# POOL's subtraction for k in two halves; pair 2's centroid steps and the products of the turned w_out one slot later

## The chip, the cores and the metric

The kernel runs on one core of one Trainium2 chip. The metric is the device time of one execution in microseconds (us); 562.74, 564.26 and 565.34 us were measured for the kernel before, and their median is the time to beat. Names of engines: PE is TensorE, DVE is VectorE, ACT is ScalarE, POOL is GpSimd, SP is SyncE, which issues all DMAs here.

## The reference

Three layers follow each other: clustered attention, a layer with a rational activation, and a soft mixture of experts.

```python
# attention: B=2, H=8, S=768, D=64, 16 centroids a head
q_assign = np.argmax(np.einsum('bhsd,hcd->bhsc', q_n, c_n), axis=-1)     # and k_assign
mask = q_assign[:, :, :, None] == k_assign[:, :, None, :]
scores = np.where(mask, scale * np.matmul(q, k.transpose(0, 1, 3, 2)), -1e9)
attn = softmax(scores);  x = attn @ v                                    # -> [1536, 512]
# rational layer: d_ff = 2048
h = x @ w_in;  g = (a0 + a1*h + a2*h2 + a3*h3) / (1 + |b0|*|h| + |b1|*h2 + 1e-6);  x = g @ w_out
# soft mixture: 8 experts of 4 slots, F = 1024
logits = x @ phi;  slot_input = softmax_over_tokens(logits).T @ x
slot_out[e] = relu(slot_input[e] @ w1[e]) @ w2[e];  out = softmax_over_slots(logits) @ slot_out
```

## The kernel before

**The slots.** Attention is a loop over 96 slots, 12 for each of 8 pairs of heads (a pair is two heads of one batch, 2 x 64 rows). In slot n, PE turns (transposes) the exponentials of unit n (`turn`, L398, tile sT), then makes the scores of unit n+2 (`a1_mm`, L374 and L375, tile s), then the steps listed as "P" for this slot, then the product with v of an earlier group (`a2_av`, L411), then the steps listed as "T". DVE does its listed steps first ("D0", "D", "D1") and then the row minimum of the scores of unit n+2 (`a1_neg`, L383, tile e); ACT does the exponential of unit n+1 (L387) and copies the turned tile out (L404, eT), then its listed steps ("A"). POOL does only listed steps ("G0", "G"). Each list has (slot offset, engine, step) entries: a table written by hand sets the order on PE, ACT, DVE and POOL. The scores have one PSUM buffer, so L374 of a slot waits until DVE's L383 of the slot before has read it; sT has one too.

**The steps of a pair.** While a pair is in its 12 slots, `prep` prepares the pair two ahead; it is added at slot 4 of each pair (for pair 2 at slot 4 of the whole loop, so an entry with offset 1 stands in slot 5). `scores` (L230) multiplies raw q and k with the centroids, two halves c = 0 and 1; `scaled` (L235, ACT) scales them; `scT` (L249) turns them; `best` (L257, L258, DVE) finds the maximum; `first(0)` to `first(2)` (L266, L268, L271, DVE) make a one-hot (eq); `ohT`, `count`, `masks`, `nonhot`, `signed` and `alive` (L276, L284, L290 to L293, L298, L303, L311) make masks from it, and `qalive` (L315, DVE) applies one to q. `ksplit` rounds k on POOL (L239, ka) and subtracts the rounded part (L240, kb); six DMAs (L244) bring ka and kb to the operand tiles k1 and k2. `qsplit` (L325, L326) does the same with q.

**Small PSUM tiles.** All these small products, and those of the weights below, take tiles mf of one pool with three buffers (`m_tile`); a product that finds its buffer unread waits on its engine, and everything behind it on that engine waits too.

**The weights.** 32 blocks of w_in and w_out are decoded from 64-bit floats meanwhile (`decode_steps`: L521, L522, L528, L532 on DVE, L525 on ACT, L537 and L544, L545 on POOL). For each of the 16 blocks of w_out, `wphi_steps` turns the block (`tr`, L560), copies it (`tcopy`, L564, tile wT, ACT), multiplies it with phi (`mm`, L569), keeps the result (`keep_`, L576, DVE), and for every fourth block turns and sums it (`fin`, L581; `total`, L584). Blocks start every 2.65 slots.

**Start and fillers.** Pair 0 is prepared ahead of slot -2 (`first_pair`). There the centroid norms end with L502 and L503 on DVE (tile pc), on which L235 waits. Products with a tile of zeros (`idle`, L478, tile rest) fill PE there and in slots up to 5.

**The rest.** L768 to L771 are the products with w_in, with the rational function on ACT, POOL and DVE; the last stage (L983 to L1074) makes the experts. There the order on PE for the experts' products is not written by hand: a scheduler orders L1074 (products with w2), L1038 (sums of slot outputs, tile SO, copied and split by DVE at L1040 and L1042) and L1049 (output products). The order of SP's DMAs is the scheduler's too.

Of the kernel before, what the change touches and what calls it, by code (L numbers as in the profile page):

```python
# [8 lines left out]
F32 = mybir.dt.float32  # L9
# [5 lines left out]
ALU = mybir.AluOpType  # L15
# [43 lines left out]
def tile_kernel(ctx, tc, qT, kT, v, cenT, cenP, consts, constsb, ab, w_in, w_out, phi, w1, w2, out, dbg=None):  # L59
    nc = tc.nc  # L60
    PE, ACT, DVE, POOL, SP = nc.tensor, nc.scalar, nc.vector, nc.gpsimd, nc.sync
# [5 lines left out]
    HS = S // 2  # L67
# [80 lines left out]
    def m_tile(dt=F32):  # L148
        if dt == BF16:
            return psM.tile([128, 1024], BF16, tag="m", name="mb")  # L150
        return psM.tile([128, 512], F32, tag="m", name="mf")

    def first_pair(r, o, f):

        hold = f["hold"]

        def nonhot_k(h):
            m = psS[h].tile([128, 2, 512], F32, tag="S", name="s1")
            for c in range(2):
                PE.matmul(m[64:80, c, 0:HS], hold["W"][0:64, 160 + 16 * h:176 + 16 * h],  # L160
                          hold["oT"][0:64, c * HS:(c + 1) * HS], start=True, stop=True)
            ACT.activation(o[h]["k2"][64:80, :].rearrange("p (c n) -> p c n", c=2), m[64:80, :, 0:HS], AF.Copy, scale=-BIG)

        def nonhot_q(h, c):
            m = m_tile()
            w = slice(c * HS, (c + 1) * HS)
            PE.matmul(m[64:80, 0:HS], hold["W"][0:64, 128 + 16 * h:144 + 16 * h], hold["oT"][0:64, w], start=True, stop=True)
            ACT.copy(o[h]["q2"][64:80, w], m[64:80, 0:HS])

        def q0(h):  # L170
            w = slice(0, HS)
            q1, q2 = o[h]["q1"], o[h]["q2"]
            a, l = slice(64 * h, 64 * h + 64), slice(64 - 64 * h, 128 - 64 * h)
            qa = hold["qa", 0]
            ACT.copy(q1[a, w], qa[a, :])
            POOL.tensor_scalar(q2[0:64, w], qa[a, :], 1.0, 1.0, ALU.mult, ALU.mult)
            DVE.tensor_tensor(q1[l, w], qa[a, :], q1[a, w].bitcast(F32), ALU.subtract)

        def front():
            f["scores"](0)  # L180
            f["scores"](1)
            f["ksplit"]()
            idle(2)
            f["scaled"](0)
            f["scT"](0)
            f["best"](0)
            f["scaled"](1)
            f["scT"](1)
            f["best"](1)
            for i in range(3):  # L190
                f["first"](i)
            idle(12)
            f["ohT"]()
            f["count"]()
            idle(8)
            f["masks"]()

        def back():
            f["alive"](0)
            f["qalive"](0)  # L200
            nonhot_k(0)
            q0(0)
            nonhot_q(0, 0)
            q0(1)
            nonhot_k(1)
            nonhot_q(1, 0)
            idle(4)

        rest = [(0, "P", lambda: f["alive"](1)),
                (1, "D", lambda: f["qalive"](1)),  # L210
                (1, "G", lambda: f["qsplit"](1, slice(HS, S))),
                (1, "P", lambda: (nonhot_q(0, 1), nonhot_q(1, 1)))]
        return front, back, rest

    def prep(p):

        hp = p % (H // 2)
        r = raws.pop(p)
# [3 lines left out]
        def tile_(pool, tag, shape, dt):  # L222
            hold[tag] = pool.tile(shape, dt, tag=tag, name=tag)
            return hold[tag]

        def scores(c):
            m = hold["m", c] = m_tile()
            for g in range(4):
                a = slice(64 * (g % 2), 64 * (g % 2) + 64)
                PE.matmul(m[32 * g:32 * g + 32, 0:HS], cT[a, hp, :], r["qqkk"[g]][a, c * HS:(c + 1) * HS],  # L230
                          start=True, stop=True)

        def scaled(c):
            sc = hold["sc"] if c else tile_(t_p, "sc", [128, S], F32)
            ACT.activation(sc[:, c * HS:(c + 1) * HS], hold.pop(("m", c))[:, 0:HS], AF.Copy, scale=rn[:, hp:hp + 1])  # L235

        def ksplit():
            ka, kb = tile_(t_p, "ka", [128, S], F32R), tile_(t_p, "kb", [128, S], F32R)
            POOL.tensor_scalar(ka, r["k"], 1.0, 1.0, ALU.mult, ALU.mult)  # L239
            POOL.tensor_tensor(kb, r["k"], ka.bitcast(F32), ALU.subtract)  # L240
            for h in range(2):
                a = slice(64 * h, 64 * h + 64)
                for dst, src in ((o[h]["k1"][0:64, :], ka), (o[h]["k1"][64:128, :], ka), (o[h]["k2"][0:64, :], kb)):
                    SP.dma_start(dst.bitcast(F32), src[a, :].bitcast(F32))  # L244

        def scT(c):
            m = hold["m", c] = m_tile()
            for i in range(3):
                PE.transpose(m[:, i * 128:(i + 1) * 128], hold["sc"][:, (3 * c + i) * 128:(3 * c + i + 1) * 128], ident)  # L249

        def best(c):
            if c == 0:
                tile_(s2_p, "mx", [128, 6, 4], F32)
                tile_(t_p, "eq", [128, 6, 4, 16], BF16)
            mv = hold.pop(("m", c))[:, 0:HS].rearrange("p (i g c) -> p i g c", i=3, g=4)[:, :, :, 0:16]
            mc = hold["mx"][:, 3 * c:3 * c + 3, :]
            DVE.tensor_reduce(mc, mv, AX.X, ALU.max)  # L257
            DVE.tensor_tensor(hold["eq"][:, 3 * c:3 * c + 3], mv,  # L258
                              mc.unsqueeze(3).to_broadcast([128, 3, 4, 16]), ALU.is_equal)
# [72 lines left out]

        if p == 0:
            return first_pair(r, o, locals())
        return [
            (1, "T", lambda: scores(0)),
            (2, "A", lambda: scaled(0)),
            (2, "T", lambda: scores(1)),
            (3, "P", lambda: scT(0)),
            (3, "A", lambda: scaled(1)),  # L340
            (4, "D0", lambda: best(0)),
            (4, "P", lambda: scT(1)),
            (5, "D0", lambda: best(1)),
            (6, "D0", lambda: first(0)),
            (6, "G", ksplit),
            (7, "D0", lambda: first(1)),
            (8, "D0", lambda: first(2)),
# [128 lines left out]
    def idle(n):  # L476
        for _ in range(n):
            PE.matmul(rest_ps, zero[:, 0:128], zero, start=True, stop=True)  # L478
# [75 lines left out]
    def wphi_steps(f):  # L554

        def steps(hold):
            def tr():
                m = hold["m"] = m_tile()
                for c in range(NCC):
                    PE.transpose(m[:, c * 128:(c + 1) * 128], hold["w"][:, c * 128:(c + 1) * 128], ident)  # L560

            def tcopy():
                hold["wT"] = dec_p.tile([128, 512], F32, tag="wT", name="wT")
                ACT.copy(hold["wT"], hold.pop("m"))  # L564

            def mm():
                m = hold["m"] = m_tile()
                for c in range(NCC):
                    PE.matmul(m[32 * c:32 * c + 32, 0:128], ph[:, c, :], hold["wT"][:, c * 128:(c + 1) * 128],  # L569
                              start=True, stop=True)  # L570

            def keep_():
                k = f % 4
                if k == 0:
                    wph["t"] = dec_p.tile([128, 512], F32, tag="wph", name="wph")
                DVE.tensor_copy(wph["t"][:, k * 128:(k + 1) * 128], hold.pop("m")[:, 0:128])  # L576

            def fin():
                m = hold["m"] = m_tile()
                for k in range(4):  # L580
                    PE.transpose(m[:, k * 128:(k + 1) * 128], wph["t"][:, k * 128:(k + 1) * 128], ident)  # L581

            def total():
                DVE.tensor_reduce(wphi0[:, f - 3:f + 1, :], hold.pop("m").rearrange("p (k c s) -> p k s c", k=4, c=4),  # L584
                                  AX.X, ALU.add)

            return [(4, "P", tr), (5, "A", tcopy), (5, "T", mm), (6, "D1", keep_)] + \
                ([(6, "P", fin), (7, "D1", total)] if f % 4 == 3 else [])
        return steps

    w_in_w = w_in.bitcast(I32)
# [40 lines left out]
    manual.__enter__()  # L632
    start()
    front, back, rest = prep(0)
    SP.dma_start(ph, phi.rearrange("(c p) s -> p c s", p=128))
    SP.dma_start(coef, ab)
    steps = prep(1)
    front()
    early = [steps.pop(0)[2] for _ in range(5)]
# [8 lines left out]
    for n in range(-LEAD, NSL + 6):  # L648
        p, k = divmod(n, 12)
# [7 lines left out]
        if k == 4 and n > 0 and p + 2 < NP:  # L657
            add(n, prep(p + 2))
# [408 lines left out]
    for c0, cw in COLS:  # L1067
        ne = 256 // cw
        so = bank()
        for e in range(E):  # L1070
            wt = W["w2", e - e % ne, c0][0][:, (e % ne) * 8 * cw:]
            for kk in range(8):
                k = kk % 4
# [77 lines left out]
```

## Time and profile before

| what | value |
|---|---|
| median of three runs | 564.26 us (562.74 to 565.34) |
| the profiled execution's own time | 561.49 us |
| its span, first to last instruction | 559.7 us |
| busy: PE, DVE, ACT, POOL | 528.1, 425.9, 380.5, 275.4 us |
| mean granted PE clock, of full speed | 0.995 |
| chain that ended last, by engine | PE 66%, DVE 19%, ACT 9% |

The span and the busy times are of the one profiled execution, which was 2.77 us faster than the median. The attention slots reach from about 20 to 306 us, the products with w_in to about 500 us, the experts to the end. A busy PE is not PE at its peak, since matmuls overlap in the records.

### The profile page before, as it was taken

The page shows a single profiled execution, that of the slowest core. Times are in us where ns is not written, and L with a number is a line of the kernel's source. Part 1 is how long each engine was busy: PE and PEld are TensorE (multiplying, and loading weights), DVE is VectorE, ACT ScalarE, POOL GpSimd, SP SyncE. Part 2 cuts the span into 40 slices and gives each one's busy share as a digit, 9 for nine tenths or more (in the row PEclk, how much of TensorE's full clock was granted, in tenths as well). Part 3 has the DMA queues.
Part 4 walks back from the last instruction along what each step waited for, and adds up shares of the span by engine and source line. Part 5 has one row for each costly group of instructions (what it writes and reads, how often), then busy time and mean ns, then how long its engine had stood idle before and what let it go on. Part 6 is the DMA issues. An engine that isn't in the chain of part 4 may idle for free.

```text
span 559.7 us, 10057 instructions
## 1 busy us (share of the span) xinstructions
PE 528.1 (94%) x3521; PEld 343.1 (61%) x3521; DVE 425.9 (76%) x801; ACT 380.5 (68%) x693; POOL 275.4 (49%) x304
## 2 busy tenths in 40 slices
PE   8989899998998999999999999999999999988994
PEld 3546556655565655665566687777677767743363
DVE  5668899788789898898853399999799996961133
ACT  2777778877887868787776488887678877840111
POOL 3445567576475665755621575555355545601000
PEclk9989999999999999999999999999999999999999
DMA  8957759687496694856540377676476756379997
GB/s 235 291 140 223 216 172 274 202 231 237 141 264 199 204 233 183 228 156 188 166 151 1 104 268 270 226 264 246 159 249 223 269 207 225 118 321 383 418 420 279
DMA packets 43282, 125.71 MB, mean 225 GB/s; under 512 B 6432, under 2 KB 7328, under 8 KB 38624
## 3 DMA queue, kind: packets, MB, share of 16 engines
q1 hardware_dynamic: 43232, 125.07, 68.4%
q8 instruction: 28, 0.46, 0.3%
q14 instruction: 22, 0.18, 0.1%
HBM read 89.66 MB, written 15.73 MB: 188 GB/s over the span
## 4 chain that ended last, share of the span: by engine, by line
PE 66%; DVE 19%; ACT 9%; issue 3%; DMA 2%; POOL 1%; DVEq 0%; ACTq 0%; POOLq 0%
PE h L768 8%; PE h L771 8%; PE h L769 8%; PE sT L398 7%; PE av L411 6%; DVE e L383 5%; DVE mh L522 4%; PE gt L829 3%; PE s L374 3%; PE s L375 3%; ACT e L387 3%; PE pb L1074 3%; PE pb L1003 2%; ACT eT L404 2%; PE l L835 2%
## 5 line engine op out<-in xcount | busy, mean ns | idle before, releaser
L387 ACT ACTIVATE e<-e,nv 128x768 f32<-128x768 f32 x96 | 89.8, 936 | 52.9 <-DVE e L383 36.3
L383 DVE TENSOR_SCALAR_CACHE_REDUCE e<-s 128x768 f32<-128x768 f32 x96 | 91.5, 953 | 37.0 <-PE s L375 34.6
L398 PEld LDWEIGHTS sT<-cst,e 128*128 128x128 f32 x576 | 61.9, 141 | 52.0 <-ACT eT L404 26.6
L398 PE MATMUL sT<-cst,e 128*128 128x128 f32 x576 | 84.0, 282 | 1.0 <-ACT eT L404 0.6
L404 ACT COPY eT<-sT 128x768 f32<-128x768 f32 x96 | 75.6, 788 | 13.2 <-PE sT L398 12.4
L374 PE MATMUL s<-k,q 128*128 128x384 f32 x192 | 73.6, 383 | 9.6 <-DVE e L383 7.2
L411 PE MATMUL av<-eT,vt 128*64 128x384 f32 x384 | 82.1, 510 | 0.0
L768 PE MATMUL h<-xh,w 128*128 128x512 f32 x192 | 80.6, 420 | 0.0
L537 POOL TENSOR_TENSOR w<-mh,ex 128x512 f32<-128x512 f32 x32 | 42.7, 1334 | 74.9 <-DVE ex L532 43.3
L769 PE MATMUL h<-xl,w 128*128 128x512 f32 x192 | 75.9, 395 | 0.0
L799 POOL TENSOR_SCALAR q<-u,babs 128x512 f32<-128x512 f32 x47 | 36.2, 770 | 73.9 <-ACT u L797 73.9
L375 PE MATMUL s<-k,q 80*128 80x384 f32 x192 | 64.9, 338 | 0.0
L801 POOL TENSOR_TENSOR q<-q,u 128x512 f32<-128x512 f32 x47 | 60.9, 1297 | 3.8
L771 PE MATMUL h<-xh,w 128*128 128x512 f32 x192 | 52.8, 396 | 0.0
L797 ACT ACTIVATE u<-h 128x512 f32<-128x512 f32 x47 | 27.9, 594 | 28.3 <-PE h L771 25.4
L768 PEld LDWEIGHTS h<-xh,w 128*128 128x128 f32 x192 | 36.2, 189 | 16.0 <-DVE p L816 3.4
L374 PEld LDWEIGHTS s<-k,q 128*128 128x128 f32 x192 | 36.4, 190 | 15.3 <-DVE e L383 11.6
L800 DVE TENSOR_TENSOR p<-p,h 128x512 f32<-128x512 f32 x47 | 32.1, 683 | 14.7 <-ACT p L798 14.6
L771 PEld LDWEIGHTS h<-xh,w 128*128 128x128 f32 x192 | 36.3, 189 | 8.9
L769 PEld LDWEIGHTS h<-xl,w 128*128 128x128 f32 x192 | 36.2, 189 | 7.2 <-issue 0.5
L808 ACT ACTIVATE r<-q,epsc 128x512 f32<-128x512 f32 (+1 forms) x49 | 33.8, 690 | 8.2 <-POOL q L801 6.7
L816 DVE SCALAR_TENSOR_TENSOR p<-p,ncoef,r 128x512 f32<-128x512 f32 (+1 forms) x49 | 35.9, 732 | 2.4 <-ACT r L809 1.8
(178 smaller groups left out, 1012.9 us busy)
## 6 DMA issues: line engine op xcount, KB each, us to landing
wt<-w SPq DMA_DIRECT2D x32, 1024.0 KB, 8.1
w<-w_in SPq DMA_DIRECT2D x96, 256.0 KB, 3.2
raw<-w_in SPq DMA_DIRECT2D x16, 512.0 KB, 4.4
raw<-w_out SPq DMA_DIRECT2D x16, 512.0 KB, 5.1
w_in<-w SPq DMA_DIRECT2D x16, 512.0 KB, 3.9
k<-ka SPq DMA_DIRECT2D x32, 192.0 KB, 6.1
q<-qh SPq DMA_DIRECT2D x28, 192.0 KB, 4.7
w_out<-w SPq DMA_DIRECT2D x16, 256.0 KB, 4.3
```

The costliest lines, as they stand in the source:

```text
L374: PE.matmul(ps[:, c, 0:HS], o["q1"][:, it], o["k1"][:, w], start=True, stop=False)
L375: PE.matmul(ps[:, c, 0:HS], o["q2"][0:80, it], o["k2"][0:80, w], start=False, stop=True)
L383: DVE.tensor_scalar(e, s1s.pop(u)[:, :, 0:HS], -1.0, None, ALU.mult, ALU.min, accum_out=nvs[g][:, rest:rest + 1])
L387: ACT.activation(es[u], es[u], AF.Exp, scale=-1.0, bias=nvs[g][:, rest:rest + 1], accum_out=sums[g][:, rest:rest + 1])
L398: PE.transpose(ps[:, j // 3, j % 3 * 128:(j % 3 + 1) * 128], e[:, j, :], ident)
L404: ACT.copy(dst, eTp.pop(u)[:, :, 0:HS].rearrange("p c (j t) -> p c j t", j=3))
L411: PE.matmul(av[g][64 * h:64 * h + 64, 0:HS], vs[g // 2][:, h, j, :], eTs[g][:, h, j, :], start=(j == 0), stop=(j == 5))
L537: POOL.tensor_tensor(w, hold["mh"].bitcast(F32), hold["ex"].bitcast(F32), ALU.mult)
L768: PE.matmul(h, wh[:, c, :], xh[t][:, c, :], start=(c == 0), stop=False)
L769: PE.matmul(h, wh[:, c, :], xl[t][:, c, :], start=False, stop=False)
L771: PE.matmul(h, wl[:, c, :], xh[t][:, c, :], start=False, stop=(c == NCC - 1))
L801: POOL.tensor_tensor(q, q, u, ALU.mult)
```

## The change

Three edits. `ksplit` makes kb in two instructions of 384 columns instead of one of 768. For pair 2 alone, `scores` to `best` stand one slot later; `first` and what follows stay. In `wphi_steps`, `mm`, `keep_`, `fin` and `total` stand one slot later; `tr` and `tcopy` stay.

```diff
         def ksplit():
             ka, kb = tile_(t_p, "ka", [128, S], F32R), tile_(t_p, "kb", [128, S], F32R)
             POOL.tensor_scalar(ka, r["k"], 1.0, 1.0, ALU.mult, ALU.mult)
-            POOL.tensor_tensor(kb, r["k"], ka.bitcast(F32), ALU.subtract)
+            for c in range(2):
+                w = slice(c * HS, (c + 1) * HS)
+                POOL.tensor_tensor(kb[:, w], r["k"][:, w], ka[:, w].bitcast(F32), ALU.subtract)
...
+        b = 1 if p == 2 else 0
         return [
-            (1, "T", lambda: scores(0)),
+            (1 + b, "T", lambda: scores(0)),
...
-            (5, "D0", lambda: best(1)),
+            (5 + b, "D0", lambda: best(1)),
             (6, "D0", lambda: first(0)),
             (6, "G", ksplit),
...
-            return [(4, "P", tr), (5, "A", tcopy), (5, "T", mm), (6, "D1", keep_)] + \
-                ([(6, "P", fin), (7, "D1", total)] if f % 4 == 3 else [])
+            return [(4, "P", tr), (5, "A", tcopy), (6, "T", mm), (7, "D1", keep_)] + \
+                ([(7, "P", fin), (8, "D1", total)] if f % 4 == 3 else [])
```

The rows of order below show line numbers of the kernel they come from; in the changed kernel the lines behind the edits stand two or three further down (L374 is L377, L311 is L313, L1049 is L1052).

PE in slots 5 and 6 of the kernel before: W_134 and oT are masks of pair 1, rawq and rawk are raw operands of pair 2.

```order
L311 LDWEIGHTS W_134
L311 MATMUL mf<-oT,W_134 128x384
L230 MATMUL mf<-rawq,cT 32x384 x2
L230 MATMUL mf<-rawk,cT 32x384 x2
L478 LDWEIGHTS zero
L478 MATMUL rest<-zero 128x512
...
L398 MATMUL sT<-cst,e 128x128 x6
L374 MATMUL s_576<-k_0_0_119,q_0_0_117 128x384
```

The same place of the changed kernel, up to the second of the two `alive` products and what follows it:

```order
L313 LDWEIGHTS W_134
L313 MATMUL mf<-oT,W_134 128x384
L481 LDWEIGHTS zero
L481 MATMUL rest<-zero 128x512
...
L401 MATMUL sT<-cst,e 128x128 x6
L377 MATMUL s_571<-k_0_0_119,q_0_0_117 128x384
...
L313 LDWEIGHTS W_134
L313 MATMUL mf<-oT,W_134 128x384
L414 MATMUL av<-eT,vt 64x384 x2
L230 MATMUL mf<-rawq,cT 32x384 x2
L230 MATMUL mf<-rawk,cT 32x384 x2
```

The first half of pair 2's `scores` (L230) has gone from between `alive` and the fillers of slot 5 to the end of slot 6; the second half has gone from slot 6 to slot 7.

PE near the end of the kernel before, where the scheduler orders the experts' products; SO is a sum that DVE has copied:

```order
L1074 MATMUL pb<-wt,HZ 32x128 x16
L1038 MATMUL pb<-SO,cst 128x128
L1049 MATMUL pb<-cT_6021,SO_6234 128x512 x3
L1074 MATMUL pb<-wt,HZ 32x128 x48
```

And of the changed kernel:

```order
L1077 MATMUL pb<-wt,HZ 32x128 x21
L1041 MATMUL pb<-SO,cst 128x128
L1077 MATMUL pb<-wt,HZ 32x128 x11
L1052 MATMUL pb<-cT_6029,SO_6242 128x512 x3
L1077 MATMUL pb<-wt,HZ 32x128 x32
```

Sixteen of the 48 products that stood behind the three output products now stand ahead of them: five before L1041 and eleven between it and L1052.

## Rows read from the trace of the kernel before

**Rows 1.** Busy time of stretches: PE, PEld, DVE, ACT, POOL, PEclk, DMA share, GB/s.
```profile
0.00:20.00 20.00, 17.12 (x94) 7.36 (x95) 10.65 (x30) 7.71 (x15) 8.37 (x18) 1.00 0.92 268
20.00:306.00 286.00, 269.09 (x1778) 169.49 (x1778) 232.29 (x456) 219.83 (x407) 161.88 (x181) 0.99 0.66 193
```
**Rows 2.** Waits of PE from 20 to 306 us: total, times, longest.
```profile
PE s L374 <- DVE e L383: 7.2, 11, 1.0
...
PE mf L230 <- DVE qa L315: 1.3, 1, 1.3
PE mf L569 <- ACT wT L564: 1.3, 4, 0.4
```
**Rows 3.** Timeline of PE, slots 5 and 6: start, length, instruction, idle before.
```profile
37.01 0.34 PE L311 MATMUL mf<-oT,W 80*128 80x384 bf16 x1
38.70 0.85 PE L230 MATMUL mf<-rawq,cT 64*32 64x384 f32 x2 [1.35 <-DVE qa L315]
...
41.38 1.07 PE L398 MATMUL sT<-cst,e 128*128 128x128 f32 x6
```
**Rows 4.** Busy time and granted clock (PEclk) of a stretch there.
```profile
38.70:41.40 2.70, 2.70 (x12) 0.72 (x13) 0.89 (x1) 1.71 (x4) 2.01 (x3) 0.50 0.57 196
```
**Rows 5.** Timeline, same place: ACT, DVE and a DMA issue of SP.
```profile
37.16 0.78 ACT L404 COPY eT<-sT 128x768 f32<-128x768 f32 x1
...
38.09 0.55 DVE L315 SCALAR_TENSOR_TENSOR qa<-rawq,mf 128x384 f32<-128x384 f32 x1
...
43.20 0.96 DVE L383 TENSOR_SCALAR_CACHE_REDUCE e<-s 128x768 f32<-128x768 f32 x1 [3.60 <-PE s L375]
...
49.40 0.60 SPq L331 DMA_DIRECT2D q<-qh  x1
```
**Rows 6.** Line L331, the DMAs of q: time from issue to landing.
```profile
DMA to landing us min/median/max: 3.3/4.9/8.1
```
**Rows 7.** Timeline, slots 10 and 11, POOL, DVE and PE.
```profile
53.96 1.83 POOL L240 TENSOR_TENSOR kb<-rawk,ka 128x768 fp32r<-128x768 f32 x1
...
53.98 2.02 DVE L266 TENSOR_TENSOR eq<-eq,cb 128x384 bf16<-128x384 bf16 x1
...
57.95 0.44 PE L374 MATMUL s<-k,q 128*128 128x384 f32 x1 [0.93 <-DVE e L383]
```
**Rows 8.** Lines L240, L266 and L326: ns min/median/max of one.
```profile
L240 POOL TENSOR_TENSOR kb<-rawk,ka x8: 1808/1829/2143, 6.2 to 234.9; 128x768 fp32r<-128x768 f32 x8
...
L266 DVE TENSOR_TENSOR eq<-eq,cb x8: 348/1155/2027, 11.0 to 238.1; 128x384 bf16<-128x384 bf16 x8
...
L326 POOL TENSOR_TENSOR ql<-qa,qh x15: 1000/1008/1325, 24.6 to 263.8; 128x384 fp32r<-128x384 f32 x15
```
**Rows 9.** Timeline: two POOL instructions in a row, one of DVE across them.
```profile
69.38 0.62 POOL L544 TENSOR_SCALAR w<-w 128x512 fp32r<-128x512 f32 x1
69.58 0.69 DVE L521 TENSOR_SCALAR ex<-raw 128x512 int32<-128x512 int32 x1
...
70.08 1.33 POOL L545 TENSOR_TENSOR w<-w,w 128x512 fp32r<-128x512 f32 x1
```
**Rows 10.** Timeline of the start: DVE and PE.
```profile
6.33 1.68 DVE L502 TENSOR_SCALAR pc<-pc 128x4 f32<-128x4 f32 x1
...
8.95 1.02 PE L249 MATMUL mf<-cst,sc 128*128 128x128 f32 x6 [0.68 <-ACT sc L235]
```
**Rows 11.** Timeline of PE: waits behind three other L266.
```profile
101.88 0.44 PE L374 MATMUL s<-k,q 128*128 128x384 f32 x1 [0.72 <-DVE pres L290]
...
129.96 0.45 PE L374 MATMUL s<-k,q 128*128 128x384 f32 x1 [0.52 <-DVE e L383]
...
204.66 0.44 PE L374 MATMUL s<-k,q 128*128 128x384 f32 x1 [0.92 <-DVE e L383]
```
**Rows 12.** Timeline of PE near the end.
```profile
548.39 0.94 PE L1049 MATMUL pb<-cT,SO 128*128 128x512 f32 x3 [1.10 <-DVE SO L1042]
549.26 2.83 PE L1074 MATMUL pb<-wt,HZ 128*32 128x128 f32 x96
```

More of the change, by code (lines that the diff above doesn't have):

```diff
@@ L334, in prep @@
             return first_pair(r, o, locals())
+        b = 1 if p == 2 else 0
         return [
-            (1, "T", lambda: scores(0)),
[L337 to L342, printed above, removed]
-            (5, "D0", lambda: best(1)),
+            (1 + b, "T", lambda: scores(0)),
+            (2 + b, "A", lambda: scaled(0)),
+            (2 + b, "T", lambda: scores(1)),
+            (3 + b, "P", lambda: scT(0)),
+            (3 + b, "A", lambda: scaled(1)),
+            (4 + b, "D0", lambda: best(0)),
+            (4 + b, "P", lambda: scT(1)),
+            (5 + b, "D0", lambda: best(1)),
             (6, "D0", lambda: first(0)),
```

## The prediction

> **What bounds the kernel now.** I read four views in this order: busy time by stage, the waits of PE, the timeline around each wait that the three edits touch, and the chain that ended last. From 20 to 306 us PE is busy for 269.09 of 286 us, DVE for 232.29 and POOL for 161.88 [rows 1]. So PE is nearly full, and time there can be won in two ways only: less work for PE, or shorter waits. The change takes no product away; it can win waits alone. PE waits about 17 us in this stretch by the difference. The largest share is L374, the scores, which wait for DVE's row minimum L383 (7.2 us in 11 waits); L569, the product with phi, waits four times for ACT's copy (1.3 us in all), and one L230 waits 1.3 us for L315 [rows 2]. The reader should see that each of the three edits aims at one of these lines.
>
> **Slot 5: the moved scores of pair 2.** PE finishes `alive` at 37.01 + 0.34 = 37.35 us and then stands at the first L230 of pair 2 until 38.70 [rows 3]. What released it is L315 on DVE, which ends at 38.09 + 0.55 = 38.64 [rows 5]: the product takes the small PSUM buffer that this `qalive` reads. Behind L230 on PE stand the fillers, then sT of slot 6, which starts at 41.38 only. The wait costs more than its 1.35 us. After it the granted clock is 0.50, that is 1.2 GHz, from 38.70 to 41.40 [rows 4]; 2.70 us at half clock hold 1.35 us of work at full clock. Together 1.35 + 1.35 = 2.7 us.
>
> In the changed kernel the fillers follow `alive` at once, and sT of slot 6 can start when ACT has copied the sT before, at 37.16 + 0.78 = 37.94 [rows 5], instead of 41.38. The second `alive` takes over the wait for L315, but it now stands behind sT and the scores of slot 6, so PE comes to it later than 38.64. The moved L230 come at the ends of slots 6 and 7, where their inputs are old; their work is not saved, only moved. I take 2.7 us. The bounds: 0 if an equal wait takes its place, 41.38 - 37.94 = 3.4 us if nothing else is late.
>
> What is late next there? The scores of pair 1, in slots 10 and 11, need pair 1's q. Its last DMA is issued at 49.40 and lands, with the median of 4.9 us of that line, at about 54.3 [rows 5, 6] (an estimate). Before, the scores of slot 11 start at 57.95 [rows 7]; with 2.7 us off they would start at 55.25, still behind the landing, even if the DMA gains nothing. So SP's queue does not take it back. `best(1)` now stands in slot 10 ahead of `first(0)` on DVE; its place in slot 9 is empty instead, so DVE does the same work, and L266 cannot start before POOL lets it anyway (next part).
>
> **kb in two halves.** kb occupies POOL for 1.83 us at 53.96. DVE's L266 starts at 53.98 and takes 2.02 us [rows 7], though one that is left alone takes 0.348 [rows 8]. It ends 0.2 us behind kb. L266, L383 behind it, and PE's L374 behind that are late in a row: PE waits 0.93 us at 57.95 [rows 7]. A subtraction of 384 columns, L326, takes 1.008 us against 1.829 for kb [rows 8]. If DVE gets in between the halves, L266 ends 0.82 us sooner. That it does is suggested by a place where two POOL instructions stand back to back: L521 starts under L544 and ends at 70.27, just behind the end of L544 (70.00), while L545 runs on to 71.41 [rows 9].
>
> What PE gets of it is the smaller of 0.82 and its wait: 0.82 at 57.95 [rows 7], 0.72 at 101.88 (there through a load that was issued behind a late L266), 0.52 at 129.96 and 0.82 at 204.66 [rows 11]; 2.9 us. Behind the other L266 I count nothing. Some of it will be met by the next limit in the same slot, so I take four fifths, 2.3 us. The bounds are 0 (DVE does not get in) and 2.9. POOL itself pays 2 x 1.008 - 1.829 = 0.19 us eight times, 1.5 us, beside 124 us in which it is idle [rows 1]: nothing. The DMAs of kb come 0.2 us later, with a whole pair's time before they are read; the scheduler puts the h = 0 part behind ka's in SP's queue, which costs the same.
>
> The Trainium skill has a rule on this, in SBUF — State Buffer, section Who interferes with whom: DVE and GpSimd share a port pair as an exclusive lock for a whole instruction, and issue order decides who blocks. Read strictly it speaks against the edit: if the second half is issued before DVE has the pair, L266 waits for both halves. The trace agrees on the whole instruction: L266 ended 0.2 us behind kb. By the strict reading the sum would be 4.35 us instead of 7.0; the place above where DVE came between two POOL instructions speaks for the other outcome.
>
> **The start.** L502 on DVE, an instruction on 4 columns, takes 1.68 us from 6.33, under pair 0's kb; PE's L249 then waits 0.68 us for ACT's scaling, which needs it [rows 10]. Half of kb gives up to 0.82 here, of which PE can take 0.68. But the DMA share up to 20 us is 0.92 [rows 1], so much there may be late through loads that do not move. I take 0.35; bounds 0 and 0.68.
>
> **The products of the turned weights.** L569 one slot later finds the copy of the slot before, so its 1.3 us of waits [rows 2] go. The 16 x 4 products stay, and the PSUM tile of the copy is free as before. The wait has to be on the path to count, which at four places it mostly is, as PE is full. I take 1.0; bounds 0 and 1.3. Keeping and summing one slot later have nobody waiting until the products with w_in.
>
> **The end.** The scheduler now puts 16 of the last products ahead of L1049, 11 of them between L1038 and L1049. Before, PE waits 1.10 us there for DVE's split; the products are two records each, 96 records in 2.83 us [rows 12], so 11 of them fill 22 x 2.83 / 96 = 0.65 us of the wait. The other five only change places. The last output products come 0.65 us sooner. Bounds 0 (if weights for them came late; PE shows no such wait there) and 0.65.
>
> **The sum.** 2.7 + 2.3 + 0.35 + 1.0 + 0.65 = 7.0 us. Against the profiled execution's 561.49 us this is 554.5; that execution stands 2.77 us below the median of 564.26, so the median should come to 557.3 us. All upper bounds together are 3.4 + 2.9 + 0.68 + 1.3 + 0.65 = 8.9, that is 555.3 by the median.
>
> **The rivals.**
> First: the waits in slots 5 to 11 come back elsewhere. For it: L374 waits for DVE in 11 places already, and PE cannot outrun DVE, busy 81% of this stretch [rows 1]. Against it: DVE itself idles for 3.60 us here, as its next row minimum at 43.20 waits for scores that stand behind L230 on PE [rows 5]. Then the 2.7 fall away: 564.26 - 4.3 = 560.0 us. Chance 0.13.
>
> Second: DVE does not get in between the halves; the parts of 2.3 and 0.35 go to nothing: 564.26 - 4.35 = 559.9 us. Chance 0.14. First and second together leave 1.65 us: 562.6, no change that can be told. Chance 0.07.
>
> Third, the other side: two POOL instructions hold DVE up twice, L266 under the first half and the DVE instruction after it under the second. Its place is the one L266 of each of five pairs. The price can be up to a second half, 1.0 us, on top of the 0.82 not won. It turns the kernel slower only when five pairs lose together what slot 5, L569 and the end win (4.35) and 2.8 more: 7.2 / 5 = 1.4 us each. With 1.5 each the time is 564.26 - 4.35 + 7.5 = 567.4 us. L521 in [rows 9] speaks against it, for it was held once. Chance 0.04.
>
> **How the numbers follow.** The forecast has 0.62, with a range of its own from 554.5 to 559.5 us. A measurement of this kernel tells about 0.5%, 2.8 us, from no change: faster means below 561.4. The forecast and the first two rivals alone lie there, 0.62 + 0.13 + 0.14, of which I take 0.03 off for runs near the edge: 0.86 faster; 0.10 same; 0.04 slower. The range reaches from 553.8 (all upper bounds, and 1.5 us more for two other holds of DVE of 0.82 us that fall away as instructions shift in time) to 561.0, which takes in the first two rivals with 1 us to spare.
>
> **What would show it.** Right: no PE wait over 0.3 us at L230 in slot 5, a granted clock of 1.0 from 38 to 42 us, sT of slot 6 near 38 us instead of 41.38 [rows 3]; L266 at most 1.2 us where it was 2.02; no wait of L569 on ACT; 0.45 us instead of 1.10 at L1049. Wrong: a PE wait over 1 us in slots 6 to 12 with a clock of 0.5 behind it, or L266 still near 2 us, ending behind the second half.

## The result, and the profile after

The changed kernel takes 557.15 us (median of 4 runs, 556.02 to 559.51), beside 563.5 us for the kernel before, timed with it: ratio 0.9892, 95% interval 0.9845 to 0.9939, so 6.1 us faster (3.4 to 8.7). Timed a second time it gave 0.9902 (0.9869 to 0.9934), 5.5 us. The forecast was 557.3 us with a gain of 7.0; the time fits better than the gain does, because the median of 564.26 from which it was counted lay above the medians that before had later (562.1 to 563.5). The time of an execution goes with its mean granted clock: of 67 executions of before timed beside the experiments, the ten at 0.998 took 560.9 us on the mean, the 17 at 0.995, where the profiled one stands, 562.4, and the ten at 0.989 took 565.7.

The profiled execution took 557.32 us, its span is 555.4. Where it won time is read from the start of `turn` (sT) in each slot, after minus before: +0.14 us in slot 0, +0.13 in slot 5, -2.16 in slot 6, -1.56 in slot 11, -2.74 in slot 15, -3.31 in slot 36, -3.84 in slot 48, -3.89 in slot 94. So nothing at the start, 2.3 us in slot 5, and the rest in small steps and losses. Of the 2.3 us 2.1 are left at sT of slot 8 (-1.92), behind the products that moved to slots 6 and 7.

The waits of PE from 20 to 306 us, the view of [rows 2] (L377 is L374 of before, L386 its L383):

```profile
PE s L377 <- DVE e L386: 7.7, 10, 1.3
PE mf L300 <- DVE W L295: 2.8, 6, 0.8
PE s L377 <- DVE pres L292: 1.7, 2, 1.3
```

L230 and the product with phi have gone from the list, as two of the edits meant. The wait for the row minimum has not shrunk (7.2 before), and its longest is now 1.3 us. It stands in slot 5. The timeline of PE there, which answers to [rows 3], and the stretch of [rows 4]:

```profile
37.41 0.44 PE L377 MATMUL s<-k,q 128*128 128x384 f32 x1 [1.30 <-DVE e L386]
...
38.22 0.34 PE L313 MATMUL mf<-oT,W 80*128 80x384 bf16 x1
38.40 0.81 PE L481 MATMUL rest<-zero 128*128 128x512 bf16 x3
39.22 0.88 PE L401 MATMUL sT<-cst,e 128*128 128x128 f32 x6
...
38.70:41.40 2.70, 2.69 (x18) 1.57 (x16) 2.38 (x5) 2.70 (x5) 1.40 (x2) 1.00 0.46 190
```

The wait of 1.35 us at L230 is gone and one of 1.30 us stands at L377, yet sT of slot 6 starts at 39.22 instead of 41.38: the L230 products, which filled PE from 38.70 to 40.13 us in the kernel before, stand elsewhere, and the granted clock is 1.00 (2.4 GHz) where it was 0.50. What made L386 late is seen on DVE and POOL just ahead:

```profile
34.64 0.41 DVE L524 TENSOR_SCALAR ex<-raw 128x512 int32<-128x512 int32 x1
34.98 1.50 DVE L525 TENSOR_SCALAR mh<-raw 128x512 int32<-128x512 int32 x1
36.41 0.94 DVE L386 TENSOR_SCALAR_CACHE_REDUCE e<-s 128x768 f32<-128x768 f32 x1
...
34.80 1.41 POOL L540 TENSOR_TENSOR w<-mh,ex 128x512 f32<-128x512 f32 x1 [9.06 <-DVE ex L535]
```

L525 and L524 do the same kind of work, and one took 0.41 us, the other 1.50: L540 began 0.18 us ahead of L525, and L525 ended 0.27 us behind it. POOL could begin because DVE's L535, the instruction ahead of L524, had just set it free. In the kernel before the same pair (L522 and L537 there) met the other way round, DVE's instruction left alone and POOL's long:

```profile
34.66 1.73 POOL L537 TENSOR_TENSOR w<-mh,ex 128x512 f32<-128x512 f32 x1 [9.06 <-DVE ex L532]
...
34.84 0.41 DVE L522 TENSOR_SCALAR mh<-raw 128x512 int32<-128x512 int32 x1
```

kb, DVE at pair 5's place, which answers to [rows 7], and the lengths of L268 (L266 of before) and L531 (L528), which answer to [rows 8]:

```profile
123.08 2.09 POOL L242 TENSOR_TENSOR kb<-rawk,ka 128x384 fp32r<-128x384 f32 x2
...
123.11 1.20 DVE L268 TENSOR_TENSOR eq<-eq,cb 128x384 bf16<-128x384 bf16 x1
124.23 1.49 DVE L531 SCALAR_TENSOR_TENSOR mh<-raw,mh 128x512 f32<-128x512 uint32 x1
125.64 0.94 DVE L386 TENSOR_SCALAR_CACHE_REDUCE e<-s 128x768 f32<-128x768 f32 x1
...
126.65 0.44 PE L377 MATMUL s<-k,q 128*128 128x384 f32 x1 [0.50 <-DVE e L386]
...
L268 DVE TENSOR_TENSOR eq<-eq,cb x8: 347/395/1201, 11.1 to 233.6; 128x384 bf16<-128x384 bf16 x8
...
L531 DVE SCALAR_TENSOR_TENSOR mh<-raw,mh x32: 643/686/1487, 29.9 to 277.3; 128x512 f32<-128x512 uint32 x32
```

DVE does get in between the halves: L268 takes 1.20 us instead of 2.03. But the second half then holds L531, which takes 1.49 us where its median is 0.69. DVE wins 0.82 and loses 0.80, and PE waits 0.50 us at 126.65 where it waited 0.52 at 129.96 [rows 11].

At the start and at the end, answering to [rows 10] and [rows 12]:

```profile
6.15 0.84 DVE L503 SCALAR_TENSOR_TENSOR pc<-pc 128x4 f32<-128x4 f32 x1
7.03 0.92 DVE L504 SCALAR_TENSOR_TENSOR pc<-pc 128x4 f32<-128x4 f32 x1
...
9.10 1.02 PE L251 MATMUL mf<-cst,sc 128*128 128x128 f32 x6 [0.67 <-ACT sc L235]
...
544.92 0.94 PE L1052 MATMUL pb<-cT,SO 128*128 128x512 f32 x3 [0.32 <-DVE SO L1045]
```

In place of one instruction of 1.68 us (L502 of before) the two ahead of it now take 0.84 and 0.92 us, one under each half, and PE waits 0.67 us as before (0.68). At the end the wait has fallen from 1.10 to 0.32.

### The profile page after: what moved, and what is told of

Same layout as the page of the kernel before. It is cut to its first block, busy times and chain, and to the rows that moved or that the text cites. A ratio compares the mean times of both kernels' runs of the same rounds, so it can differ in the third digit from the quotient of the medians.

```text
span 555.4 us, 10060 instructions
## 1 busy us (share of the span) xinstructions
PE 526.7 (95%) x3518; PEld 342.8 (62%) x3521; DVE 425.8 (77%) x801; ACT 380.1 (68%) x693; POOL 277.5 (50%) x312
## 4 chain that ended last, share of the span: by engine, by line
PE 68%; DVE 19%; ACT 7%; issue 2%; DMA 2%; DVEq 0%; POOL 0%; ACTq 0%
PE h L771 8%; PE h L774 8%; PE h L772 8%; PE av L414 7%; PE sT L401 7%; DVE e L386 6%; PE s L377 4%; PE gt L832 3%; DVE mh L525 3%; PE s L378 3%; PE pb L1077 3%; PE pb L1006 3%; PE l L838 2%; PE mf L230 2%; ACT e L390 2%
## 5 line engine op out<-in xcount | busy, mean ns | idle before, releaser
L386 DVE TENSOR_SCALAR_CACHE_REDUCE e<-s 128x768 f32<-128x768 f32 x96 | 91.4, 952 | 35.1 <-PE s L378 28.6
L377 PE MATMUL s<-k,q 128*128 128x384 f32 x192 | 73.5, 383 | 9.9 <-DVE e L386 7.7
L540 POOL TENSOR_TENSOR w<-mh,ex 128x512 f32<-128x512 f32 x32 | 42.1, 1314 | 70.2 <-DVE ex L535 33.6
L377 PEld LDWEIGHTS s<-k,q 128*128 128x128 f32 x192 | 36.4, 190 | 14.7 <-DVE e L386 11.8
```

Source lines behind the costliest of these rows:

```text
L377: PE.matmul(ps[:, c, 0:HS], o["q1"][:, it], o["k1"][:, w], start=True, stop=False)
L386: DVE.tensor_scalar(e, s1s.pop(u)[:, :, 0:HS], -1.0, None, ALU.mult, ALU.min, accum_out=nvs[g][:, rest:rest + 1])
L540: POOL.tensor_tensor(w, hold["mh"].bitcast(F32), hold["ex"].bitcast(F32), ALU.mult)
```

## The experiments

All times are medians; the gain is (1 - ratio) times the median of before timed beside it, with its 95% interval; the difference of the two medians lies up to 1.7 us from it.

| kernel | us | ratio to before | gain, us |
|---|---|---|---|
| halves of kb alone | 562.67 | 1.0001 (0.9974 to 1.0028) | 0.0 (-1.6 to 1.5) |
| pair 2 alone | 558.84 | 0.9931 (0.9907 to 0.9956) | 3.9 (2.5 to 5.2) |
| products alone | 560.94 | 0.9972 (0.9948 to 0.9997) | 1.6 (0.2 to 2.9) |
| pair 2 and products | 558.31 | 0.9908 (0.9871 to 0.9944) | 5.2 (3.2 to 7.3) |
| the change again | 557.14 | 0.9902 (0.9869 to 0.9934) | 5.5 (3.7 to 7.4) |
| before, wait filled | 562.46 | 0.9983 (0.9954 to 1.0012) | 1.0 (-0.7 to 2.6) |
| before, no kb | 560.01 | 0.9956 (0.9936 to 0.9976) | 2.5 (1.3 to 3.6) |
| the change, sign last | 552.84 | 0.9805 (0.9767 to 0.9844) | 11.0 (8.8 to 13.1) |
| before, sign last | 553.81 | 0.9842 (0.9802 to 0.9882) | 8.9 (6.6 to 11.2) |
| sign last, kb whole | 552.62 | 0.9812 (0.9772 to 0.9851) | 10.6 (8.4 to 12.8) |
| sign last, kb after norms | 549.75 | 0.9772 (0.9734 to 0.9809) | 12.8 (10.8 to 15.0) |
| sign last, kb on DVE | 552.40 | 0.9807 (0.9760 to 0.9853) | 10.9 (8.3 to 13.5) |

**The parts by themselves.** The theory after the reading was that the halves win nothing, since the next DVE instruction pays; the rival was the forecast's own sum.

The halves alone, against before:

```diff
-            POOL.tensor_tensor(kb, r["k"], ka.bitcast(F32), ALU.subtract)
+            for c in range(2):
+                w = slice(c * HS, (c + 1) * HS)
+                POOL.tensor_tensor(kb[:, w], r["k"][:, w], ka[:, w].bitcast(F32), ALU.subtract)
```

> Only the two halves of kb; the other two edits undone. Theory A (the terms of the forecast): DVE gets in between the halves and PE keeps what L266 wins, 2.3 us at four places and 0.35 us at the start, so about 2.65 us faster than before. Theory B (read from the trace after): the instruction of DVE behind L266 is held under the second half (L531 took 1.49 us three times where 0.64 is its least), which gives back what L266 wins, and the start wins nothing: 0 to 0.8 us faster, no difference that can be told. L266 itself at most 1.2 us by both.

Measured: no gain, and the interval shuts out 2.65 us. Over the whole profile the eight L268 take 5.90 us, where the eight L266 of before took 9.44, yet DVE is busy for 426.4 us beside 425.9. The timeline of this kernel, DVE and PE at the same place, shows the exchange again (L530 is L528 of before, L376 its L374):

```profile
126.52 1.20 DVE L268 TENSOR_TENSOR eq<-eq,cb 128x384 bf16<-128x384 bf16 x1
127.64 1.49 DVE L530 SCALAR_TENSOR_TENSOR mh<-raw,mh 128x512 f32<-128x512 uint32 x1
...
130.06 0.44 PE L376 MATMUL s<-k,q 128*128 128x384 f32 x1 [0.50 <-DVE e L385]
```

Pair 2's steps alone, shown by one of its eight entries:

```diff
-            (1, "T", lambda: scores(0)),
+            (1 + b, "T", lambda: scores(0)),
```

> Only pair 2's centroid steps one slot later (the order of the last experts' products changes with it, 11 of them in the wait for SO). Theory A: the wait of L230 and the half clock behind it go, 2.7 us, and 0.65 us at the end: 3.35 us faster. Theory B: the wait partly comes back at the scores of slot 5, because DVE's L522 or the like is held under a POOL instruction there: between 1.5 and 2.7 us faster, of which about 0.4 us at the end. A rival, that the clock and not the wait is the cost, is told by sT of slot 6: with the wait back but the clock at 1.00 it still starts over 1 us sooner.

Measured: 3.9 us, as theory A has it (3.35), above theory B's range, into which its interval reaches. In its profile sT of slot 6 starts 2.06 us sooner than before although it starts 0.24 later in slot 0, so 2.3 us in slot 5, with theory B's wait of 1.30 us at the scores and a clock of 1.00, as in the change. That is the sign of the rival on the clock, though L230's own work has left slot 5 too. Part of the 3.9 us is the clock of these executions, which the edit may or may not have set: 0.9967 on the mean beside 0.9942. Where it is 0.997 or more, six executions took 558.7 us on the mean beside 560.9 for nine of before, 2.2 us less.

The products alone:

```diff
-            return [(4, "P", tr), (5, "A", tcopy), (5, "T", mm), (6, "D1", keep_)] + \
-                ([(6, "P", fin), (7, "D1", total)] if f % 4 == 3 else [])
+            return [(4, "P", tr), (5, "A", tcopy), (6, "T", mm), (7, "D1", keep_)] + \
+                ([(7, "P", fin), (8, "D1", total)] if f % 4 == 3 else [])
```

> Only the products of the turned output weights one slot later. Theory A: the four waits of L569 on ACT go, 1.0 us (at most 1.3) faster, within what can be told from nothing. Theory B: these waits go, but the next wait of PE in the same slots takes them, 0 to 0.5 us. Theory C: most of what the change won after slot 11 (sT went from 1.6 us ahead in slot 11 to 4 us ahead in slot 53) is this edit, which then is worth about 2 us.

Measured: 1.6 us, between A and C, and not far enough from either to choose. L569's waits are gone from its profile; waits for the row minimum are 11.1 us there in place of 7.2, so in that one execution part of the gain went to the next wait (its time is 561.04 beside 561.49). With the clock at 0.997 or more, six of its executions are only 0.3 us ahead of the nine of before.

Both without the halves, that is the two diffs above together:

> The change without the halves of kb. Theory A: 2.3 + 0.35 us of the gain are missing, so about 4.35 us faster than before and 2.65 us slower than the change. Theory B: the halves are worth nothing, so as fast as the change within 1 us, 557 to 558.5 us beside 563.5 for before.

Measured: 5.2 us, the change 5.5, as theory B has it. The interval (3.2 to 7.3) does not shut out theory A's 4.35 us by itself; the halves alone do.

> The changed kernel once more, as it is, timed beside the next three, since its first ratio came from four runs. Expected 0.989 of before within 0.003, that is 6 us faster. By the sum of the parts timed alone (0 for the halves, 3.9 for pair 2, 1.6 for the products) it would be 5.5 us.

Measured: 5.5 us; the parts add up, 0.0 + 3.9 + 1.6.

**The wait and the clock.** The kernel before, PE kept busy while L230 waits:

```diff
+        if n == 5:
+            idle(6)
         run(n, "T")
-        if n < 6:
+        if n < 5:
```

> The kernel before with one thing moved: the three fillers of slot 5 stand ahead of the first L230 of pair 2 and not behind it, and three more with them, so that PE is busy while L230 waits for L315. The order of all other work is that of before, so the wait stays for what stands behind L230. Theory A (half of the 2.7 us was the clock): the granted clock stays at 1.00 from 38.7 to 41.4 and sT of slot 6 starts near 39.2 us instead of 41.38, as in the change, which then owes its gain in slot 5 to the clock and to the fillers' place, not to the wait; about 2 us faster than before. Theory B (the wait itself is the cost): sT of slot 6 starts at 40 us or later and the time is within 1.4 us of before.

Measured: 1.0 us (-0.7 to 2.6), and sT of slot 6 started at 40.66, the numbers of theory B. But it isn't the comparison that was meant: L522 was held as in the change, and the scores of slot 5 waited 1.30 us, not L230. The clock did stay at 1.00, as theory A has it:

```profile
37.37 0.45 PE L374 MATMUL s<-k,q 128*128 128x384 f32 x1 [1.30 <-DVE e L383]
...
38.70:41.40 2.70, 2.65 (x21) 1.19 (x19) 1.78 (x4) 2.70 (x5) 1.40 (x2) 1.00 0.47 190
```

With a wait almost as long as before and three fillers more, slot 5 was still 0.8 us shorter. That points to the clock, but two things differ; the kernel with only the sign moved (below) has one difference.

The kernel with the products alone has both waits in slot 5, at full clock (PE, and the stretch of [rows 4]):

```profile
37.33 0.45 PE L374 MATMUL s<-k,q 128*128 128x384 f32 x1 [1.31 <-DVE e L383]
...
39.84 0.51 PE L230 MATMUL mf<-rawq,cT 64*32 64x384 f32 x2 [1.34 <-DVE qa L315]
...
41.28 0.82 PE L398 MATMUL sT<-cst,e 128*128 128x128 f32 x6
...
38.70:41.40 2.70, 1.56 (x13) 0.63 (x14) 1.73 (x4) 2.70 (x6) 1.40 (x2) 1.00 0.48 194
```

So do the kernels with the halves alone (1.20 and 1.35 us) and without kb (1.31 and 1.35), there with a clock of 0.50 behind. The wait at the scores is thus not L230's wait come back: pair 2 has not moved in these three, and in each the instruction on the bits (L522 of before) was held for 1.5 us. From sT of slot 5 to sT of slot 6 it is 6.13 us with the products alone and 3.98 with pair 2 moved alone, both with the wait at the scores and a clock of 1.00: the move takes 2.15 us out of slot 5 without any help of the clock, L230's wait and its own work of 0.8, which stands in a later slot.

**kb left out.** The kernel before without the subtraction:

```diff
-            POOL.tensor_tensor(kb, r["k"], ka.bitcast(F32), ALU.subtract)
```

> The kernel before without the subtraction for kb at all; the DMA takes ka in its place, so this part of the product of q and k is wrong. No DVE instruction can be held under kb. Theory A (L266's hold was on the path, and the change lost it because the next instruction is held by the second half): 2.3 to 3.6 us faster than before. Theory B (the hold was covered: the next limit of PE in those slots takes what L266 gives): under 1.2 us, and the waits of PE at the scores there stay over 0.5 us.

Measured: 2.5 us, theory A, at its lower end. So kb on POOL was on the path, and the forecast of what its holds cost (2.65 us) was fair; halving kb did not lift them. Leaving kb out also takes 16 us of work from POOL (275.4 to 259.2 us busy), and what that alone is worth stays open. The first sT starts 0.73 us sooner here.

**The hold that was left.** If DVE is held by POOL instructions that start just ahead of its own, the place to look is not kb but the 12 instructions on the bits (L525) that lost about 1.09 us each, ten of them under L540. What sets L540 free is the sign (L535), which stood ahead of the bits:

```diff
-        return [(-3, "S", dma), (0, "D1", bits), (1, "A", expo), (1, "D1", mant), (2, "D1", sign),
+        return [(-3, "S", dma), (0, "D1", bits), (1, "A", expo), (1, "D1", mant), (2, "D2", sign),
```

> The changed kernel with one entry moved: the sign of a weight block stands last of DVE's listed steps of its slot, behind the bits of the next block, so that POOL's product, which the sign sets free, no longer starts 0.1 us ahead of the second instruction on the bits. In the trace after, that instruction (L525) was held by about 1.09 us in 12 places. Theory A (the shared port is what makes DVE late, and DVE's row minimum is what PE waits for, 7.7 us): DVE's busy time up to 302 us falls by about 10 us, PE gets 2 to 4 us, 554 to 556 us. Theory B (PE is full and takes waits of DVE from its slack): DVE's busy time falls but the time stays within 1 us of the change.

Measured: 552.84 us, 5.5 us by the ratios below the change (11.0 - 5.5; 4.3 by the medians), more than theory A had said. The stretch from 20 to 302 us of the change, and of this kernel with L525's lengths, its waits, and DVE at the place in slot 5:

```profile
20.00:302.00 282.00, 266.62 (x1777) 168.93 (x1777) 232.24 (x456) 219.48 (x406) 163.94 (x187) 1.00 0.68 195
...
L525 DVE TENSOR_SCALAR mh<-raw x32: 414/845/1508, 28.1 to 275.7; 128x512 int32<-128x512 int32 x32
```

```profile
20.00:302.00 282.00, 270.99 (x1802) 172.87 (x1804) 225.63 (x458) 222.03 (x409) 168.43 (x193) 1.00 0.69 198
...
L525 DVE TENSOR_SCALAR mh<-raw x32: 406/422/1518, 27.1 to 268.2; 128x512 int32<-128x512 int32 x32
...
PE s L377 <- DVE e L386: 3.1, 6, 1.0
...
33.43 0.41 DVE L525 TENSOR_SCALAR mh<-raw 128x512 int32<-128x512 int32 x1
33.76 0.68 DVE L535 SCALAR_TENSOR_TENSOR ex<-raw,ex 128x512 int32<-128x512 int32 x1
34.37 0.94 DVE L386 TENSOR_SCALAR_CACHE_REDUCE e<-s 128x768 f32<-128x768 f32 x1
...
34.52 1.27 POOL L540 TENSOR_TENSOR w<-mh,ex 128x512 f32<-128x512 f32 x1 [9.74 <-DVE ex L535]
...
37.18 0.88 PE L401 MATMUL sT<-cst,e 128*128 128x128 f32 x6
...
L386 DVE TENSOR_SCALAR_CACHE_REDUCE e<-s x96: 937/957/959, 18.8 to 291.2; 128x768 f32<-128x768 f32 x96
```

DVE is busy 6.6 us less (theory A: about 10) while PE does more in the same time, and the median L525 has halved. Of the 32 L540, 17 now start under the row minimum L386 (10 in the change), two L525 are still long under L540 where it was ten, and no L386 of the 96 is held (937 to 959 ns). In slot 5 neither wait is left: sT of slot 6 starts at 37.18.

The same move on the kernel before, with none of the three edits:

> The kernel before with the sign of a weight block last of DVE's listed steps, and none of the three edits. Theory A: what it wins is apart from the three edits, about 5 us (0.991 of before), and slot 5 keeps its wait at L230 and the half clock behind it. Theory B: on the changed kernel it won by clearing slot 5 and little else (sT of slot 6 came from 2.2 us ahead to 4.2 us ahead); then it is worth under 3 us here.

Measured: 8.9 us, more than either theory. By these numbers it is worth more alone than the whole change, and the two together (11.0) less than their sum (5.5 + 8.9 = 14.4); with intervals of about 2 us on each, how much of what they win is the same stays open. Its slot 5 is the comparison that was missing, for PE and the stretch of [rows 4]:

```profile
38.77 0.51 PE L230 MATMUL mf<-rawq,cT 64*32 64x384 f32 x2 [1.34 <-DVE qa L315]
...
40.21 0.82 PE L398 MATMUL sT<-cst,e 128*128 128x128 f32 x6
...
38.70:41.40 2.70, 2.63 (x20) 1.69 (x21) 1.20 (x2) 2.13 (x5) 2.01 (x3) 1.00 0.47 187
```

The wait is that of before, at the same place and as long, the order on PE too; only the clock behind it differs, 1.00 instead of 0.50, and sT of slot 6 starts at 40.21 instead of 41.38. Theory A was right that the wait stays and wrong that the half clock does, in this execution. It has a half clock elsewhere, from 506.1 to 509.5 us, and its mean clock is 0.995 like that of the profiled execution of before, so the 8.9 us are not won by the clock of slot 5.

Three more on top of the sign. kb whole again (without the first diff above):

> The version with the sign last, but kb in one instruction again. Theory A (the halves give back what they win): as fast as with the halves within 1.5 us, 551 to 554 us. Theory B (the halves were worth something that the other holds hid): 2 us slower or more, with waits of PE over 0.5 us behind L266.

Measured: 552.62 us, theory A; the halves are worth nothing here either.

kb behind the norms, for pair 0:

```diff
+            if p == 0:
+                gate = s2_p.tile([128, 6], F32, tag="nv", name="gate", bufs=3)
+                POOL.tensor_scalar(gate[:, 0:NH], rn, 1.0, 1.0, ALU.mult, ALU.mult)
```

> The version with the sign last, and for pair 0 alone a POOL instruction on 128 x 4 that reads the centroid norms stands ahead of the halves of kb, so that they begin when DVE's small instructions there are done. Theory A (the hold at the start is on the path, as leaving kb out showed with 0.73 us): the first sT starts as soon as with kb left out or up to 0.3 us sooner than in the version with the sign last (22.75 - 0.82 = 21.93), and the time falls by up to 0.5 us. Theory B: kb comes too late for its DMA and the first scores wait for it; the first sT starts later than 22 us.

Measured: 549.75 us, the fastest of all, but its interval overlaps that of the sign alone, and in its profile the first sT starts at 22.67, not 21.93. The wait of PE for the scaling is gone there, as it should be; the first L230 waited instead for the DMA of q:

```profile
7.07 0.51 PE L230 MATMUL mf<-rawq,cT 64*32 64x384 f32 x2 [1.07 <-DMA rawq<-qT]
```

Four of its six executions have a mean clock of 0.997 or more, two of the six with the sign alone. Whether it beats the version with the sign last is open.

kb on DVE, one slot later (the subtraction stands in a step of its own, and its two DMAs with it):

```diff
+            if p:
+                DVE.tensor_tensor(kb, r["k"], ka.bitcast(F32), ALU.subtract)
...
+            (7, "D2", klow),
```

> The version with the sign last, with kb made by DVE, one slot later, for all pairs but the first; POOL only rounds. DVE pays one instruction of 768 columns a pair, an estimate of 0.9 us from the row minimum of as many columns (0.95), seven times: 6 us; it no longer is held under kb (4 us in all in the version with the sign last, 7 us in the change). Theory A (only DVE's sum counts): 0 to 2 us slower than with the sign last. Theory B (a hold costs more than work of the same length, since it falls at any place, and this work stands where DVE has time): equal or up to 2 us faster.

Measured: 552.40 us, equal within about 2.5 us, which theory B says and theory A's lower end allows. DVE pays 0.95 us a pair and gets as much back: from 20 to 302 us it is busy for 223.5 us beside 225.6.

## Why the prediction was right, and where it was not

**The bound** was read rightly: PE is full, and only waits could be won. **Slot 5**, 2.7 us, measured 2.3 in two kernels, 2.1 behind the moved products. Its two halves were sized rightly for the execution that was read: the half clock alone cost 41.38 - 40.21 + 0.08 = 1.25 us (1.35 forecast; 0.08 is what the kernel with the moved sign was behind in slot 5), and where neither wait is left, slot 5 is shorter by 4.20 - 0.67 = 3.5 us (0.67 is what that kernel was ahead in slot 5), about the upper bound of 3.4. What was missed is what else is late there. The text looked at the DMA of pair 1's q, several slots on; late was the row minimum of the same slot, behind an instruction on the bits that POOL held. In the trace of the change this looks like the first rival come partly true, but the same wait stands in three kernels where pair 2 has not moved: it came on its own, beside the gain, which is L230's wait and, in the execution of before that was read, the half clock behind it. That the half clock stands in slot 5 in every execution of before is not shown.

**The halves of kb**, 2.3 us, and **the start**, 0.35, are the terms that failed: 0.0 us measured, and sT of slot 0 is 0.14 us later. The failed step is "If DVE gets in between the halves, L266 ends 0.82 us sooner", from which the sum took the gain of one instruction for the gain of DVE. The third rival had the mechanism, the hold under the second half, but asked only whether it makes the kernel slower, and gave it 0.04; at a price equal to the gain it makes the two terms nothing, which is the time of the second rival (559.9 us by the forecast's count) for another reason. The row said to speak against it, L521 in [rows 9], was read one row too short. The next row of the trace of before is L522, under L545 of [rows 9]:

```profile
70.19 1.50 DVE L522 TENSOR_SCALAR mh<-raw 128x512 int32<-128x512 int32 x1
```

It takes 1.50 us; the same instruction takes 0.41 at 34.84. The trace of before already showed that what comes behind pays for the second POOL instruction.

The Trainium skill, in SBUF — State Buffer, section Who interferes with whom, says that the shared ports are locked for a whole instruction, and that issue order decides who blocks. The runs agree, with L531 at 1.49 us behind L268 at 1.20. Read strictly in the forecast it took the halves to be worth nothing, for the reason that L266 waits for both; the halves are worth nothing, but because two instructions wait for one half each. It also leaves the form of `tensor_scalar` that writes out its accumulator out of the operations that can take the shared ports. L386 is that form, and 937 to 959 ns in 96 instructions agree; that it reads its operand from PSUM may be the reason too, and no run here tells the two apart.

**The products**, 1.0 us, measured 1.6 (0.2 to 2.9): right within what can be told; the 0.3 us at like clock lies within its bounds too. **The end**, 0.65: the wait fell by 0.78, and from the start of the 32 products ahead of it (545.79 before, 541.90 after) to the last output products (554.10 and 549.74) it is 8.31 and 7.84 us, so 0.47.

The measured sum is 5.5 to 6.1 us against 7.0; the two failed terms are 2.65 of it, and pair 2 with the end (3.9 against 3.35) and the products (1.6 against 1.0) came out a little above theirs. That the time fell within 0.2 us of the forecast is luck: the median that it was counted from lay high by about as much as the gain was short.

## What to carry to other kernels

When a POOL instruction holds DVE, cutting it in two can move the hold to the next DVE instruction, as here: read the row behind the one that you free, and ask what else is in the queue. It wins more to look at what sets the POOL instruction free and to place that signal so that POOL starts under a DVE instruction that it doesn't hold, which here was one entry of a table and 5 to 9 us. A median of an instruction twice its minimum (L525, 845 against 414 ns), over 32 of them, is the mark to look for.

## What was not expected of the hardware

The granted clock fell to 0.50 behind a wait of 1.35 us at L230 in the kernel before, and stayed at 1.00 behind a wait of 1.34 us at the same place with the same order on PE, once the sign had moved. In both, PE was busy 1.1 to 1.2 us of the 1.35 ahead of the wait. Behind the same wait it fell to 0.50 with the halves alone and without kb, and stayed at 1.00 with the products alone. What decides it stays open, and with one trace of each kernel so does how often it falls there, so a wait on PE has a price of its own length or about 1.25 us more.

Which of two engines is held turns on very little: POOL's product began 0.15 us behind DVE's first instruction on the bits in the kernel before, and 0.16 us behind it in the change; the first time POOL waited (1.73 us), the second time DVE (1.50 us).
